# An adaLN block with linear attention and a bilinear GLU on one core: normalised q tiles 5 to 16 turned by VectorE from contiguous runs

## The chip, the cores and the metric

The kernel runs on one core of one Trainium2 chip. The metric is the device time of one execution in microseconds (us); the median of three timed runs of the kernel before is 558.22 us (558.07 to 559.64). Besides, one execution was recorded by the hardware profiler. Engines are named as the profile has them: PE is TensorE (PEld its weight loads), DVE VectorE, ACT ScalarE, POOL GpSimd, SP SyncE, whose queue issues all DMAs of this kernel.

## The reference, cut to what matters

One sequence of S = 2048 tokens with D = 512 columns, 32 heads of 16 columns, F = 1376 hidden columns of the FFN, all in float32:

```python
mod = (silu(c) @ w_mod).reshape(1, 6, 1, -1)          # sa, ca, ga, sb, cb, gb
h = layernorm(x) * (1 + ca) + sa
q, k, v = heads(h @ wqkv)
phi = lambda t: where(t > 0, t + 1, exp(t)) + 1e-6
kv = einsum("bhsd,bhse->bhde", phi(k), v);  z = phi(k).sum(s)
o = (phi(q) @ kv) / (phi(q) . z + 1e-6)
x = x + ga * (o @ wo)
h = layernorm(x) * (1 + cb) + sb
x = x + gb * (((h @ w_gate) * (h @ w_up)) @ w_down)
```

## The kernel before

**Tiling.** The 2048 tokens are 16 tiles of 128 (index i from 0 to 15), four tiles a chunk (`ch`, `NJ` = 4). A tile is 128 tokens on the partitions and 512 columns; the column blocks of 128 are k = 0 to 3 (`KD`). Nearly every buffer is one of 94 of 2 KB a partition (`NB`); of the eight PSUM banks four are of the kind `acc`, four `bank`. Every product is made from a high and a low part of each operand (fp32r), high x high + high x low + low x high, so a product over 512 rows is 12 matmuls of 512 columns.

**Order.** The order of the instructions is written by hand (`manual_schedule`): each engine works its own queue in the order in which the program issues. A helper that is called earlier stands earlier in the queues of all engines that it uses; a `move_in` or `load` stands in SP's queue.

**Stages.** (1) The first layer norm, the modulation and a loop over the 16 tiles that makes k, phi(k) and the sums over the tokens; q products (`proj(i, wq)`) are put between: tiles 0 to 3 in steps 3, 4, 6 and 7, tiles 4 and 5 at the end, tiles 6 to 11 around the matrices that follow. (2) Out of the sums come `wp`, a 512 x 512 matrix that holds k's sums, v and wo and takes phi(q) to the attention's output, and `zb`, the sum of phi(k), broadcast over the partitions. (3) For each tile: `q_a` (ACT) and `q_b` (DVE) make phi(q) (`phq`); `den_p` and `den_r` multiply it by zb and sum each head (`den_a` is both); `den_b` takes a chunk's reciprocals; `den_c` normalises the tile. Then the normalised tile has to be turned, so that its columns lie on the partitions: it is the stationary operand of the product with wp in `y_a`. `turn_h` and `turn_l` make the high and the low part of the turned tile, `y_seed` puts x into a PSUM bank, `y_a` adds 12 matmuls to it, `y_b` takes the sum out, with the statistics of the second norm. `y_step(i)` issues y_a(i), the parts of tile i + 1, the next seed and y_b(i - 1). (4) The FFN: three lone blocks of hidden columns (`gate_up`, `down`), then 18 steps of `block` (seven products `p1`, `p5`, `p6`, `p2`, `p7`, `p3`, `p4`, by sums and differences of token chunks, `Left`, and of weight blocks, `Right`, so that seven products do for eight). `ffn` is a generator; `fill(n)` lets it issue n products. While the first steps run, tiles 14 and 15 are still on their way.

**How a tile is turned.** Tiles 0 to 7: `turn_a`, four TensorE transposes into a PSUM bank (L672). Tiles 8 to 15 (`FLIPPED`): `ready` normalises a tile and stores it to memory (`move_out`), `move_in` loads it again in four pieces so that each partition has what lies in its 32 x 32 blocks, and `turn_v` transposes the 32 x 32 blocks on VectorE (L722). A block takes every fourth word of a row; so the rows of wp for these tiles are those with the same remainder by four (`wp4`), which are made by storing wp to memory (`wp_store`) and loading it in another order (`wp_fetch`). The second norm's chunks 2 and 3 go the same way (`stow`, `unstow`, `flip`, `flipped`), with scales `cb4`, `sb4` and gate and up weights `wg_4`, `wu_4` in that order of rows.

**Names that the change and the prediction touch.** L196 and L197 are the high part (ACT) and the low part (DVE or POOL) of a split; L201 is `split_raw`. L209 to L211 are the matmuls of `product`. L672 is the TensorE transpose, L676 and L680 are turn_h and turn_l, L722 is turn_v, L745 is an extra matmul that opens the bank in y_seed(8, bank), L746 the seed, L755 the matmuls of y_a, L763 and L229 the two halves of y_b for chunk 3. L601 is den_c. L824 is the eviction of `down` on DVE. L896 is flip. L1026 is a matmul of `block`; L1031 is `copy`, by which a block's product starts from another (`copy(b, a)` after p1, without which p6 can't begin). L994 are the sums of Right, L1005, L1008 and L1012 its high and low parts.

Of the kernel before, what the change touches and what calls it, by code (L numbers as in the profile page):

```python
# [11 lines left out]
ALU = mybir.AluOpType  # L12
# [12 lines left out]
def tile_adaln_block(  # L25
# [32 lines left out]
    wu_v = w_up.rearrange("(k p) f -> p k f", p=P)  # L58
    wg_4 = w_gate.rearrange("(p k) f -> p k f", p=P)
    wu_4 = w_up.rearrange("(p k) f -> p k f", p=P)  # L60
    wm_v = w_mod.rearrange("(p k) n -> p k n", k=KD)
# [8 lines left out]
    def f32(ap):  # L70
        return ap.bitcast(F32)
# [141 lines left out]
    def cut(pair, a, b):  # L213
        return pair[0][:, a:b], pair[1][:, a:b]


    class Norm:
# [38 lines left out]
        def xhat(self, *js):  # L256
            for j in js:
                self.n[j] = B("n")
                nc.scalar.activation(self.n[j], self.tiles[j], AF.Identity,  # L259
                                     scale=self.rstd[:, j:j + 1], bias=self.nmr[:, j:j + 1])  # L260

# [239 lines left out]
    for i in range(NT):  # L501
# [13 lines left out]
        if i == 2:  # L515
            turn_x()
            wq.extend(split_raw(r) for r in raw_q)
        if fresh:
# [48 lines left out]
    pzs = {}  # L567
    den0 = consts.tile([P, NH], F32, name="den0")

    def den_z():  # L570

        nc.vector.reduce_sum(den0, zb.rearrange("p (h i) -> p h i", i=DH), axis=AX.X)
        nc.vector.tensor_scalar(den0, den0, EPS_PHI, EPS_DEN, op0=ALU.mult, op1=ALU.add)

    def den_p(ch, *js, on=None):
        for j in js:
            pzs[ch, j] = B("f")
            (on or nc.gpsimd).tensor_tensor(pzs[ch, j], phq[ch * NJ + j], zb, op=ALU.mult)

# [12 lines left out]
    def den_b(ch):  # L592
        nc.vector.tensor_tensor(dens[ch], dens[ch], den0.unsqueeze(1).to_broadcast([P, NJ, NH]), op=ALU.add)
        nc.vector.reciprocal(dens[ch], dens[ch])
# [91 lines left out]

    FLIPPED = range(8, NT)
    SUMS = (0, 1, 2)
    wp4, moved = [], {}

    def wp_store():
        to = [tc.dram_tile([D, D], F32, name=f"wp_{part}") for part in range(2)]
        for g in range(KD):
            for part in range(2):
                nc.sync.dma_start(to[part][g * P:(g + 1) * P], f32(wp[g][part]))
        wp4.append(to)

    def wp_fetch():
        rows = [x.rearrange("(p k) d -> p k d", k=KD) for x in wp4.pop()]
        for k in range(KD):  # L700
            wp4.append((B("w", dt=F32R), B("w", dt=F32R)))
            for part in range(2):
                nc.sync.dma_start(f32(wp4[k][part]), rows[part][:, k])

# [14 lines left out]
    def turn_v(i):  # L719

        tps[i] = B("f")
        nc.vector.transpose(tps[i].rearrange("p (s m i) -> p m s i", m=NQ, i=BL),  # L722
                            moved.pop(i).rearrange("p (m i s) -> p m s i", m=NQ, i=BL))

# [15 lines left out]
    def y_seed(i, of=acc_bank):  # L740

        yps[i] = of()
        if of is bank:

            nc.tensor.matmul(yps[i], wp[0][0][:, :P], wp[0][0], start=True, stop=True)  # L745
        nc.scalar.activation(yps[i], xts[i // NJ][i % NJ], AF.Copy)  # L746

    def y_a(i):
        if i not in yps:
            y_seed(i)  # L750
        pq = pqs.pop(i)
        for k in range(KD):
            (ah, al), (bh, bl) = cut(pq, k * P, (k + 1) * P), (wp4 if i in FLIPPED else wp)[k]
            for x, y in ((ah, bh), (ah, bl), (al, bh)):
                nc.tensor.matmul(yps[i], x, y, start=False, stop=k == KD - 1 and x is al, skip_group_check=True)  # L755
# [10 lines left out]
    def y_step(i, *more, late=(), q=None, turn=True, seed=acc_bank):  # L766
# [6 lines left out]
        if i + 1 in tps:  # L773
            turn_h(i + 1)
            turn_l(i + 1)
        if seed is acc_bank and i + 1 < NT:
            y_seed(i + 1, seed)
# [96 lines left out]

    def by_fours(col, name):

        t, v = consts.tile([P, KD], F32, name=name), tc.dram_tile([D], F32, name=name + "_row")
        nc.sync.dma_start(v.rearrange("(k p) -> p k", p=P), col)
        nc.sync.dma_start(t, v.rearrange("(p k) -> p k", k=KD))
        return t  # L880

    def stow(ch, *js):
# [11 lines left out]
    def flip(ch, *js):  # L894
        for j in js:
            nc.vector.transpose(wide[:, j].rearrange("p (m s i) -> p m s i", m=NQ, i=BL),  # L896
                                blocks.pop((ch, j)).rearrange("p (m i s) -> p m s i", m=NQ, i=BL))

    def flipped(ch, *ks):
        for k in ks:  # L900
            f = B("f")
            nc.scalar.activation(f.rearrange("p (x i) -> p x i", i=BL),
                                 wide.rearrange("p j (m s i) -> p (j m) s i", m=NQ, i=BL)[:, :, k],
                                 AF.Identity, scale=cb4[:, k:k + 1], bias=sb4[:, k:k + 1])
            blocks[ch, "f", k] = f
# [9 lines left out]
    kept = [[tc.dram_tile([P, D], F32, name=f"kept_{ch}_{k}") for k in range(KD)] for ch in PLAIN]  # L915
    cb4, sb4 = by_fours(cb, "cb4"), by_fours(sb, "sb4")
    for ch in range(NCH):
# [62 lines left out]
    class Right:  # L980


        def __init__(self, f, plain):
            f0, self.n = fts[f]
            self.up, self.low = self.tile("raw"), self.tile("raw")
            for t, kh in ((self.up, 0), (self.low, 1)):
                for i, v in enumerate((wg_v, wu_v) if plain else (wg_4, wu_4)):
                    nc.sync.dma_start(t[:, i], v[:, kh * KH:(kh + 1) * KH, f0:f0 + self.n])
# [144 lines left out]
    def right_load(n):  # L1133
        if n < len(steps):
            rights[n] = Right(steps[n][1], steps[n][0][0] in PLAIN)

# [112 lines left out]
    den_a(2, 0, on=nc.vector)  # L1249
    den_c(6)  # L1250
    split_down(f1, nc.gpsimd)
# [34 lines left out]
    ready(12, 13)  # L1286
    g()
    y_step(11, lambda: move_in(12), turn=False, seed=False)
    y_b(11)
# [9 lines left out]
    norm2[2].nmr_of()  # L1299
    norm2[2].xhat(0, 1)  # L1300
    turn_l(12)
    first[0].sum("s1", "s3", on=nc.gpsimd)
    g(lambda: turn_v(13))
    y_seed(13, y_bank)
    norm2[2].xhat(2, 3)
    turn_h(13)
# [44 lines left out]
    fill(1)  # L1351
    norm2[3].xhat(0)
    fill(1)
    norm2[3].xhat(1)
    fill(1)
    norm2[3].xhat(2)
    stow(3, 0, 1)
    fill(1)
    norm2[3].xhat(3)
    stow(3, 2)  # L1360
# [54 lines left out]
```

## Time and profile before

| | before |
|---|---|
| timed runs, median of 3 | 558.22 us (558.07 to 559.64) |
| the profiled execution, whole | 559.39 us |
| its span, first to last instruction | 557.7 us |
| granted TensorE clock, mean | 0.997 |
| instructions | 7356 |

The span is what the profile's views divide; the rest of an execution's time lies around it. A group's row gives how often an instruction ran, its busy time, the mean of one, and the idle time of its engine just before it with what ended it. A window's row gives for each engine its busy time and, in brackets, its number of instructions, then the granted clock, the DMA share and GB/s. A chain's or a timeline's row begins with the start and the duration in us.

### The profile page before, as it was taken

What the parts mean: (1) busy time and instruction counts of PE and PEld (TensorE: products, weight loads), DVE (VectorE), ACT (ScalarE), POOL (GpSimd) and SP (SyncE); (2) the same over time, 40 slices, a digit from 0 to 9 for tenths busy, and PEclk for the clock granted to TensorE, in tenths of its full rate; (3) what the DMA queues carried; (4) which work ended last, traced back from release to release, by engine and by line L of the source; (5) the groups of instructions that cost most, each with busy time, mean ns of one, the idle gap of its engine ahead of it and who ended that gap; (6) DMA issues with size and microseconds to landing.
All of it is one profiled execution on the core that took longest, in us unless ns stands there. A gap on an engine that the chain in (4) does not pass through costs nothing.

```text
span 557.7 us, 7356 instructions
## 1 busy us (share of the span) xinstructions
PE 550.1 (99%) x2505; PEld 451.3 (81%) x2505; DVE 377.8 (68%) x605; ACT 291.4 (52%) x539; POOL 203.0 (36%) x203
## 2 busy tenths in 40 slices
PE   8999999999999999999899999999999999999997
PEld 6888888888888878878688888887888888888886
DVE  7896968977947886877877587886553544434435
ACT  3695856646477567566683545554444444444110
POOL 2000000101012300055698666566667446446200
PEclk9899999999999999999999999999999999999999
DMA  8900203220532605846435162591335222100004
GB/s 279 384 16 2 75 25 103 101 76 1 155 100 92 188 20 169 264 143 162 132 75 148 42 201 65 188 318 29 113 114 150 59 56 58 56 21 0 1 0 150
DMA packets 59141, 60.39 MB, mean 108 GB/s; under 512 B 8608, under 2 KB 37536, under 8 KB 59104
## 3 DMA queue, kind: packets, MB, share of 16 engines
q1 hardware_dynamic: 59104, 59.93, 34.3%
q8 instruction: 19, 0.31, 0.2%
q14 instruction: 18, 0.15, 0.1%
HBM read 43.65 MB, written 16.26 MB: 107 GB/s over the span
## 4 chain that ended last, share of the span: by engine, by line
PE 92%; DVE 3%; ACT 2%; DMA 1%; issue 1%; SPq 0%; DVEq 0%; ACTq 0%
PE bank L1026 32%; PE acc L1106 6%; PE acc L1107 6%; PE acc L1108 6%; PE acc L755 5%; PE bank L209 5%; PE bank L211 5%; PE bank L210 5%; PE acc L351 3%; PE acc L349 3%; PE acc L350 3%; PE bank L839 2%; PE bank L837 2%; PE bank L838 2%; PE bank L272 2%; DMA x<-in_A_x_dram 1%
## 5 line engine op out<-in xcount | busy, mean ns | idle before, releaser
L1026 PE MATMUL bank<-h,w 128*128 128x512 f32 (+1 forms) x798 | 185.4, 390 | 1.5 <-ACT bank L1031 1.5
L1026 PEld LDWEIGHTS bank<-h,w 128*128 128x128 f32 (+1 forms) x798 | 148.1, 186 | 35.8 <-ACT bank L1031 2.6
L1031 ACT ACTIVATE bank<-bank 128x512 f32<-128x512 f32 (+1 forms) x38 | 22.1, 583 | 137.1 <-PE bank L1026 137.0
L824 DVE TENSOR_TENSOR x<-acc,x 128x512 f32<-128x512 f32 (+1 forms) x73 | 48.4, 681 | 47.4 <-PE acc L1108 47.3
L1012 POOL TENSOR_TENSOR w<-raw,w 128x256 fp32r<-128x256 f32 (+3 forms) x38 | 41.3, 1086 | 95.2 <-ACT w L1005 95.2
L1107 PE MATMUL acc<-w,kh 128*128 128x512 f32 (+2 forms) x154 | 59.6, 387 | 0.0
L1106 PE MATMUL acc<-w,kh 128*128 128x512 f32 (+2 forms) x154 | 59.6, 387 | 0.0
L1108 PE MATMUL acc<-w,kl 128*128 128x512 f32 (+2 forms) x154 | 59.5, 386 | 0.0
L197 POOL TENSOR_TENSOR w<-raw,w 128x512 fp32r<-128x512 f32 (+1 forms) x25 | 36.0, 1442 | 55.3 <-ACT w L196 28.5
L250 POOL TENSOR_TENSOR rstd<-ve,half 128x4 f32<-128x4 f32 (+1 forms) x10 | 10.8, 1080 | 120.7 <-DVE ve L249 68.0
L1012 POOL TENSOR_TENSOR w<-t,w 128x512 fp32r<-128x512 f32 (+1 forms) x38 | 49.3, 1320 | 0.0
L197 DVE TENSOR_TENSOR kl<-u,kh 128x512 fp32r<-128x512 f32 (+1 forms) x38 | 26.4, 733 | 30.2 <-ACT kh L196 30.2
L209 PE MATMUL bank<-w,h 128*128 128x512 f32 x104 | 40.8, 392 | 0.0
L211 PE MATMUL bank<-w,h 128*128 128x512 f32 x104 | 40.5, 390 | 0.0
L210 PE MATMUL bank<-w,h 128*128 128x512 f32 x104 | 40.5, 389 | 0.0
L755 PE MATMUL acc<-w,xh 128*128 128x512 f32 x120 | 37.7, 395 | 0.0
L1106 PEld LDWEIGHTS acc<-w,kh 128*128 128x128 f32 (+1 forms) x154 | 28.9, 188 | 6.0
L1108 PEld LDWEIGHTS acc<-w,kl 128*128 128x128 f32 (+1 forms) x154 | 28.9, 188 | 5.9
L1107 PEld LDWEIGHTS acc<-w,kh 128*128 128x128 f32 (+1 forms) x154 | 28.9, 188 | 5.9
L1085 DVE TENSOR_TENSOR u<-bank,u 128x512 f32<-128x512 f32 (+1 forms) x19 | 13.1, 687 | 28.9 <-PE bank L1026 22.9
L259 ACT ACTIVATE n<-x,nmr,rstd 128x512 f32<-128x512 f32 x30 | 22.9, 804 | 12.2 <-DVE nmr L254 12.2
L196 ACT ACTIVATE w<-raw 128x512 fp32r<-128x512 f32 (+2 forms) x44 | 26.3, 619 | 1.9 <-DVE raw L804 1.0
(206 smaller groups left out, 1125.1 us busy)
## 6 DMA issues: line engine op xcount, KB each, us to landing
raw<-in_w_mod_dram SPq DMA_DIRECT2D x24, 256.0 KB, 3.8
raw<-in_B_w_down_dram SPq DMA_DIRECT2D x20, 256.0 KB, 3.2
raw<-in_B_w_gate_dram SPq DMA_DIRECT2D x36, 128.0 KB, 3.7
raw<-in_B_w_up_dram SPq DMA_DIRECT2D x36, 128.0 KB, 3.6
x<-in_A_x_dram SPq DMA_DIRECT2D x16, 256.0 KB, 5.7
out_dram<-x SPq DMA_DIRECT2D x15, 256.0 KB, 2.6
raw<-in_A_wqkv_dram SPq DMA_DIRECT2D x12, 256.0 KB, 5.4
wp<-w SPq DMA_DIRECT2D x8, 256.0 KB, 3.3
```

The lines of the kernel that those rows point to most:

```text
L196: nc.scalar.activation(h, src, AF.Copy)
L197: (low or nc.vector).tensor_tensor(l, src, f32(h), op=ALU.subtract)
L209: nc.tensor.matmul(ps, ah, bh, start=i == 0, stop=False)
L210: nc.tensor.matmul(ps, ah, bl, start=False, stop=False)
L211: nc.tensor.matmul(ps, al, bh, start=False, stop=i == n - 1)
L755: nc.tensor.matmul(yps[i], x, y, start=False, stop=k == KD - 1 and x is al, skip_group_check=True)
L824: nc.vector.tensor_tensor(xt[:, a:b], dn[j][:, a:b], xt[:, a:b], op=ALU.add)
L1012: sub = lambda out, x, y: (on or nc.gpsimd).tensor_tensor(out, x, f32(y), op=ALU.subtract)
L1026: mm = lambda x, y, **kw: nc.tensor.matmul(ps, x[:, k], y, skip_group_check=True, **kw)
L1106: nc.tensor.matmul(ps, hh[:, a:b], dh[:n, c:d], start=i == 0, stop=False)
L1107: nc.tensor.matmul(ps, hh[:, a:b], dl[:n, c:d], start=False, stop=False)
L1108: nc.tensor.matmul(ps, hl[:, a:b], dh[:n, c:d], start=False, stop=i == len(hs) - 1)
```

## The change

It keeps the arithmetic and changes how tiles are turned and in which order work is issued.

- **Block order of the q columns.** The columns of the q weights are put in another order as they are split: `split_blocks` reads the 512 columns as (s, q, i) with i of 32 and writes them as (q, s, i). So phi(q) of a tile comes out with its columns in that order, and the words of a 32 x 32 block are one run of 32 (the transpose in `turn_v` and `flip` reads `(m s i)` where it read `(m i s)`). Tiles 0 to 3, which TensorE still turns, need the plain order: their q products read the weights in runs of 32 (`by_row`), 48 matmuls.
- **Tiles 4 to 7** go the way of tiles 8 to 15: ready, move_in, turn_v (`FLIPPED` now begins at 4). Their 16 TensorE transposes are gone.
- With blocks of whole runs the rows of wp are the plain ones: `wp_store`, `wp_fetch`, `wp4`, `by_fours` with `cb4` and `sb4`, `wg_4` and `wu_4` are gone: 16 + 4 DMA issues. The four tiles bring 4 + 16.
- `zq` and `den0q` are copies of zb and den0 in block order (POOL and DVE, once each), used for tiles from 4 on. The second norm's chunks 2 and 3 are written in block order by `xhat_blocks`.
- The extra matmul in `y_seed(8, bank)` is gone.
- **Order.** Chunk 1's denominators move up into y_steps 1 to 3, its normalisation between the q products of tiles 12 to 15. The parts of tile 6 (counted from 0; the seventh) stand before gate_up's rest. The first Right's sums stand ahead of y_step(11); its parts, and the parts of tiles 14 and 15 and the third sums (s3) of Left, stand ahead of the first block; the eviction of chunk 1's tiles 2 and 3 stands behind the block's fourth product.

```diff
+    def by_block(x):
+        return x.rearrange("p (s q i) -> p q s i", q=NQ, i=BL)
+    def by_row(x):
+        return x.rearrange("p (q s i) -> p s q i", q=NQ, i=BL)
+    def split_blocks(raw):
+        h, l = B("w", dt=F32R), B("w", dt=F32R)
+        view = lambda x: x.rearrange("p (q s i) -> p q s i", q=NQ, i=BL)
+        nc.scalar.activation(view(h), by_block(raw), AF.Copy)
+        nc.vector.tensor_tensor(view(l), by_block(raw), view(f32(h)), op=ALU.subtract)
+        return h, l
...
+        def xhat_blocks(self, *js):
+            for j in js:
+                self.n[j] = B("n")
+                nc.scalar.activation(self.n[j].rearrange("p (q s i) -> p s q i", q=NQ, i=BL),
+                                     self.tiles[j].rearrange("p (s q i) -> p s q i", q=NQ, i=BL), AF.Identity,
                                      scale=self.rstd[:, j:j + 1], bias=self.nmr[:, j:j + 1])
...
-        product(ps, [(cut(norm[ch].t[k], j * P, (j + 1) * P), w[k]) for k in range(KD)])
+        rows = w is wq and i not in FLIPPED
+        product(ps.rearrange("p (s q i) -> p s q i", q=NQ, i=BL) if rows else ps,
+                [(cut(norm[ch].t[k], j * P, (j + 1) * P), tuple(by_row(x) for x in w[k]) if rows else w[k])
+                 for k in range(KD)])
...
+            zq = B("z")
+            nc.gpsimd.tensor_copy(zq.rearrange("p (q s i) -> p q s i", q=NQ, i=BL), by_block(zb))
...
-    FLIPPED = range(8, NT)
+    FLIPPED = range(4, NCH * NJ)
...
         nc.vector.transpose(tps[i].rearrange("p (s m i) -> p m s i", m=NQ, i=BL),
-                            moved.pop(i).rearrange("p (m i s) -> p m s i", m=NQ, i=BL))
+                            moved.pop(i).rearrange("p (m s i) -> p m s i", m=NQ, i=BL))
...
-        if of is bank:
-
-            nc.tensor.matmul(yps[i], wp[0][0][:, :P], wp[0][0], start=True, stop=True)
...
-            (ah, al), (bh, bl) = cut(pq, k * P, (k + 1) * P), (wp4 if i in FLIPPED else wp)[k]
+            (ah, al), (bh, bl) = cut(pq, k * P, (k + 1) * P), wp[k]
...
-    y_step(1)
+    y_step(1, lambda: den_a(1, 0, on=nc.vector))
     y_step(2, lambda: split_gu(f0, nc.gpsimd))
-    y_step(3, lambda: scale_down(f0), wp_store, turn=False, seed=False)
+    den_a(1, 1, on=nc.vector)
+    y_step(3, lambda: scale_down(f0), turn=False, seed=False)
+    den_a(1, 2, 3, on=nc.vector)
+    den_b(1)
     ps12 = proj(12, wq)
     y_b(3)
     norm2[0].rstd_of()
-    den_a(1, 0, on=nc.vector)
+    ready(4)
     q_a(12, ps12)
     ps13 = proj(13, wq)
+    ready(5)
     ln2_nx(0)
     q_b(12)
-    den_a(1, 1, 2, on=nc.vector)
+    ready(6)
+    move_in(4)
     q_a(13, ps13)
     ps14 = proj(14, wq, acc_bank)
     split_down(f0, nc.gpsimd)
-    den_a(1, 3, on=nc.vector)
-    den_b(1)
+    ready(7)
+    move_in(5)
     ln2_turn(0, 0, 1, cast=nc.vector)
     q_b(13)
     ps15 = proj(15, wq, acc_bank)
     ln2_turn(0, 2, 3, cast=nc.vector)
+    move_in(6, 7)
     q_a(14, ps14)
-    den_c(4)
+    split_gu(f1, nc.gpsimd)
+    turn_v(4)
     q_b(14)
     q_a(15, ps15)
-    split_gu(f1, nc.gpsimd)
     g = gate_up(0, f0)
     q_b(15)
-    den_c(5)
+    turn_v(5)
     scale_down(f1)
     g()
-    turn(4)
+    turn_h(4)
+    turn_l(4)
     y_seed(4)
     split_gu(f2)
     g = gate_up(0, f1)
+    turn_v(6)
     den_a(2, 0, on=nc.vector)
-    den_c(6)
     split_down(f1, nc.gpsimd)
     g()
     y_step(4, lambda: scale_down(f2), lambda: den_a(2, 1, on=nc.vector))
     g = gate_up(0, f2)
     split_down(f2)
-    den_c(7)
+    turn_h(6)
+    turn_l(6)
+    y_seed(6)
+    turn_v(7)
+    g()
     den_a(2, 2, on=nc.vector)
-    g()
-    y_step(5, lambda: den_a(2, 3, on=nc.vector), wp_fetch)
+    y_step(5, lambda: den_a(2, 3, on=nc.vector))
...
+    right_sums(0, nc.vector)
     y_step(11, lambda: move_in(12), turn=False, seed=False)
...
     turn_v(14)
-    take = down(1, (2, 3))
+    down_13 = down(1, (2, 3))
     first[1].sum("s1", "s3", "s2", "s4", on=nc.gpsimd)
+    right_split(0)
     y_seed(14, y_bank)
     turn_h(14)
+    turn_v(15)
+    turn_l(14)
+    turn_h(15)
     first[0].split("s1", "s2")
-    turn_l(14)
+    first[1].split("s1", "s2")
     y_b(13)
+    turn_l(15)
+    for x in first:
+        x.split("s3")
+    right_sums(1, nc.vector)
     y_seed(15, y_bank)
-    right_sums(0, nc.vector)
-    take()
-    first[1].split("s1", "s2")
-    turn_v(15)
     for n in range(4):
         banks.append(bank())
-    banks[:] = [banks[n] for n in (2, 0, 1, 3)]
     turn_bank[0] = acc_bank
-    right_split(0)
     draw_load(0)
...
     y_step(14, seed=None)
     fill(1)
     y_b(14)
-    right_sums(1, nc.vector)
-    first[0].split("s3", "s4")
     fill(1)
-    first[1].split("s3", "s4")
+    for x in first:
+        x.split("s4")
     fill(2)
+    down_13()
     y_step(15)
```

More of the change, by code (lines that the diff above doesn't have):

```diff
@@ L259, in xhat @@
                 nc.scalar.activation(self.n[j], self.tiles[j], AF.Identity,
+                                     scale=self.rstd[:, j:j + 1], bias=self.nmr[:, j:j + 1])
+        def xhat_blocks(self, *js):
[3 more added lines that the diff above has]
+                                     self.tiles[j].rearrange("p (s q i) -> p s q i", q=NQ, i=BL), AF.Identity,
                                      scale=self.rstd[:, j:j + 1], bias=self.nmr[:, j:j + 1])
@@ L516, in tile_adaln_block @@
             turn_x()
-            wq.extend(split_raw(r) for r in raw_q)
+            wq.extend(split_blocks(r) for r in raw_q)
         if fresh:
@@ L568, in tile_adaln_block @@
     den0 = consts.tile([P, NH], F32, name="den0")
+    den0q = consts.tile([P, NH], F32, name="den0q")
     def den_z():
@@ L685, in turn @@
         turn_l(i)
-    FLIPPED = range(8, NT)
     SUMS = (0, 1, 2)
[L689 to L703, printed above, removed]
+    moved = {}
     def move_out(*tiles):
@@ L773, in y_step @@
         if i + 1 in tps:
-            turn_h(i + 1)
+            if i + 1 not in pqs:
+                turn_h(i + 1)
             turn_l(i + 1)
-        if seed is acc_bank and i + 1 < NT:
+        if seed is acc_bank and i + 1 < NT and i + 1 not in yps:
             y_seed(i + 1, seed)
@@ L873, in ln2_nx @@
         ln2_xhat(ch)
[L875 to L880, printed above, removed]
     def stow(ch, *js):
@@ L1134, in right_load @@
         if n < len(steps):
-            rights[n] = Right(steps[n][1], steps[n][0][0] in PLAIN)
+            rights[n] = Right(steps[n][1])
     def right_sums(n, on=None):
@@ L1299, in tile_adaln_block @@
     norm2[2].nmr_of()
-    norm2[2].xhat(0, 1)
+    norm2[2].xhat_blocks(0, 1)
     turn_l(12)
@@ L1304, in tile_adaln_block @@
     y_seed(13, y_bank)
-    norm2[2].xhat(2, 3)
+    norm2[2].xhat_blocks(2, 3)
     turn_h(13)
@@ L1351, in tile_adaln_block @@
     fill(1)
-    norm2[3].xhat(0)
+    norm2[3].xhat_blocks(0)
     fill(1)
-    norm2[3].xhat(1)
+    norm2[3].xhat_blocks(1)
     fill(1)
-    norm2[3].xhat(2)
+    norm2[3].xhat_blocks(2)
     stow(3, 0, 1)
     fill(1)
-    norm2[3].xhat(3)
+    norm2[3].xhat_blocks(3)
     stow(3, 2)
```

17 lines of the change are left out of this document (8 added, 9 removed).

## The prediction

> **What bounds the kernel now.** I read the engine shares first, then the share of each engine in the chain of work that ended last.
>
> ```profile
> span 557.7 us, 7356 instructions
> PE 550.1 (99%) x2505; PEld 451.3 (81%) x2505; DVE 377.8 (68%) x605; ACT 291.4 (52%) x539; POOL 203.0 (36%) x203
> PE 92%; DVE 3%; ACT 2%; DMA 1%; issue 1%; SPq 0%; DVEq 0%; ACTq 0%
> ```
>
> TensorE is busy for 550.1 of 557.7 us. A busy bar can hide a bubble, so the pace comes next: 102 matmuls in 23.22 us (chain, below) are 0.2276 us each, while one record lasts 0.39 us, because they overlap. Wherever neighbours start 0.23 us apart TensorE is full, and only two things can move the end: fewer TensorE instructions, or fewer waits in its queue. The waits of TensorE, and the last stretch:
>
> ```profile
> PE acc L148 <- DVE w L143: 2.0, 1, 2.0
> PE bank L1026 <- ACT bank L1031: 1.5, 1, 1.5
> PE bank L279 <- ACT n L259: 0.4, 1, 0.4
> 525.00:558.00 33.00, 29.09 (x135) 24.13 (x133) 15.34 (x24) 4.96 (x9) 1.29 (x1) 1.00 0.18 64
> ```
>
> The first and third waits lie in the first 20 us, and the 3.9 us without TensorE at the end are the last eviction and store; the change touches neither. One wait is left, in the first FFN block at L1026. TensorE's rows there:
>
> ```profile
> 263.59 3.19 PE L1026 MATMUL bank<-h,w 128*128 128x512 f32 x12
> 268.29 3.02 PE L1026 MATMUL bank<-h,w 128*128 128x512 f32 x12 [1.51 <-ACT bank L1031]
> 271.15 0.61 PE L755 MATMUL acc<-w,xh 128*128 128x512 f32 x2
> 274.03 23.22 PE bank L1026 x102
> ```
>
> Twelve matmuls from 263.59 at 0.2276 would let the next start at 266.32; it starts at 268.29. So the hole is 1.97 us by starts, not the 1.51 the wait shows (the last record's overhang hides the rest). The twelve after it take 2.86 us instead of 2.73, another 0.13 for filling the pipe again: **2.10 us** in all.
>
> What ScalarE and VectorE did before it:
>
> ```profile
> 243.35 0.17 DVE L247 TENSOR_SCALAR ve<-sums 128x4 f32<-128x4 f32 x1 [2.11 <-ACT acc L238]
> 256.10 1.10 DVE L722 STREAM_TRANSPOSE f<-u 128x512 f32<-128x512 f32 x1
> 258.42 1.29 DVE L197 TENSOR_TENSOR h<-s,h 128x512 fp32r<-128x512 f32 x2 [1.22 <-ACT h L196]
> 260.24 0.69 DVE L229 BATCH_NORM_STATS2 st<-acc 128x6 f32<-128x512 f32 x1
> 262.50 1.28 DVE L824 TENSOR_TENSOR x<-acc,x 128x512 f32<-128x512 f32 x2
> 263.70 2.38 DVE L197 TENSOR_TENSOR h<-s,h 128x512 fp32r<-128x512 f32 x2
> 266.00 1.08 DVE L722 STREAM_TRANSPOSE f<-u 128x512 f32<-128x512 f32 x1
> 267.12 0.63 ACT L676 ACTIVATE xh<-f 128x512 fp32r<-128x512 f32 x1 [2.61 <-DVE f L722]
> 267.66 0.58 ACT L1031 ACTIVATE bank<-bank 128x512 f32<-128x512 f32 x1
> ```
>
> The copy that TensorE waits for (L1031) had its input at about 265. It stood in ScalarE's queue behind the high part of tile 15 (L676), which waited for tile 15's VectorE transpose (L722 at 266.00), which stood behind four right-hand sums, two evictions (L824) and two low parts (L197) on VectorE.
>
> **The change part by part.**
>
> TensorE transposes of tiles 4 to 7 (L672) and the extra matmul of y_seed(8) go:
>
> ```profile
> 200.51 0.44 PE bank L672 x4
> 200.95 2.76 PE acc L755 x12
> 204.14 5.49 PE acc L755 x24
> 215.64 0.39 PE L745 MATMUL bank<-w 128*128 128x512 f32 x1
> 215.87 0.39 PE L863 MATMUL acc<-w,kh 128*128 128x512 f32 x1
> ```
>
> Four tiles at 0.44 us are 1.76; the lone matmul is the distance 215.64 to 215.87, 0.23. All 17 instructions stand in a stretch where TensorE never waits, so **1.99 us** leave its queue if its inputs keep up.
>
> The hole at 266 to 268: tile 15's transpose now stands right behind tile 14's, before all the low parts; the first right-hand sums move some 20 us ahead to y_step(11), into the 2.11 us that VectorE idles before 243.35; both evictions move behind the block's fourth product. Nothing of tile 15 stands in front of L1031 any more. What is late next is y_seed(15) on ScalarE: it waits for the statistics of tile 13 (L229), behind four low parts. From tile 14's transpose (256.10, with TensorE 1.99 earlier: 254.1) VectorE has two transposes, one low part of a tile, four L197, L229. Bounds: at quick rows (0.69, 0.69, 0.65, 0.69) 5.4 us, ending 259.5; at slow ones (1.10, and 1.19, half of the 2.38, for five low parts, which POOL's work for right_split(0) in its new place may bring) 8.8 us, ending 262.9. Seed and copy at L1031's 0.58 each add 1.2, so the copy is done between 260.7 (then its own input at 263 decides) and 264.1; TensorE needs it at 266.32 - 1.99 = 264.33. The hole closes at both ends, by little at the slow one. I take **2.10 us** gained, and a loss of up to 0.5 for a further slow row as range.
>
> VectorE now turns tiles 4 to 7, and all tiles from contiguous runs instead of every fourth word:
>
> ```profile
> L722 DVE STREAM_TRANSPOSE f<-u 128x512 f32<-128x512 f32 x8 | 8.8, 1097 | 0.0
> L197 DVE TENSOR_TENSOR w<-raw,w 128x512 fp32r<-128x512 f32 x16 | 10.5, 684 | 0.0
> L292 DVE CAST h<-f 128x512 fp32r<-128x512 f32 x19 | 8.0, 419 | 1.6 <-ACT f L284 1.6
> ```
>
> No row shows a contiguous transpose. Bounds: 0.42 us (L292, the quickest pass over 512 columns) and 1.10 (no change). I take 0.69, like every full-rate pass. The Trainium skill, Vector Engine (DVE) Microarchitecture Reference, section Measured stream behaviour on trn2, says that a port keeps full rate only on runs of at least two adjacent words, and gives 1.73 ns a column against 1.054 when one source hops every element; for 512 columns and its 75 ns an estimate from that page is 0.96 against 0.61 us. The 1.10 here fits the hopping kind roughly; the other end no run here shows yet.
>
> Does VectorE keep up with the shorter TensorE stream? The tightest place is tile 7:
>
> ```profile
> 169.07 0.17 DVE L247 TENSOR_SCALAR ve<-sums 128x4 f32<-128x4 f32 x1 [5.02 <-ACT acc L238]
> 180.50:205.70 25.20, 25.20 (x119) 19.83 (x118) 22.45 (x36) 15.20 (x31) 4.81 (x3) 1.00 0.34 104
> 180.50 0.68 DVE L317 SCALAR_TENSOR_TENSOR h<-bank,h 128x512 f32<-128x512 f32 x1
> 183.22 0.68 DVE L601 SCALAR_TENSOR_TENSOR h<-h,den 128x512 f32<-128x512 f32 x1
> 192.65 1.06 DVE L601 SCALAR_TENSOR_TENSOR h<-h,den 128x512 f32<-128x512 f32 x1
> 204.97 0.69 DVE L680 TENSOR_TENSOR xl<-bank,xh 128x512 fp32r<-128x512 f32 x1 [0.32 <-ACT xh L676]
> ```
>
> VectorE is busy 22.45 of 25.2 us here. Tile 7's low part ends at 205.66; its first user is the third matmul of y_a(7), at 204.14 + 14 x 0.229 = 207.35: 1.7 us to spare. TensorE will come 1.76 earlier. VectorE loses four normalisations from this stretch (L601, 0.68 to 1.06, at least 2.7; they move to 169 to 174, where its queue had the denominators, and those move ahead into idle time such as the 5.02 us before 169.07) and q_b(13) (0.68), and gains four transposes, 2.8 (or 4.4). Spare afterwards: 1.7 - 1.76 + 2.7 + 0.68 - 2.8 = 0.5 us, or 1.1 short if the transposes stay at 1.10. I take nothing lost, 1.1 as the other end.
>
> The way through memory: per tile one store and four loads.
>
> ```profile
> moved<-h SPq DMA_DIRECT2D x8, 256.0 KB, 2.1
> u<-moved SPq DMA_DIRECT2D x32, 64.0 KB, 2.0
> 214.82 3.72 SPq L717 DMA_DIRECT2D u<-moved  x8
> 176.95 4.61 SPq L286 DMA_DIRECT2D kept<-f  x4
> ```
>
> Twenty issues come to SyncE's queue; eight stores of wp, its eight loads and four of the column scales go. Tile 4 is normalised right behind L247 at 169.07 and stored near 170; its loads are issued behind tile 6's store, near 173, and at 0.47 us each (3.72 / 8) and 2.0 of landing are in by 177. Its transpose stands where L601 stood at 183.22, behind the modulated blocks: 6 us to spare. Tiles 6 and 7 are issued behind the kept stores, which end at 181.56; eight loads and the landing put them in by 187.3. Tile 6's transpose stands two VectorE passes ahead of its L601 at 192.65, about 191, tile 7's later. They cost nothing; were they late, VectorE's queue would be too, as under the late parts below.
>
> Strided passes elsewhere: split_blocks, xhat_blocks and zq read or write runs of 32 words.
>
> ```profile
> L902 ACT ACTIVATE f<-wide,sb,cb 128x512 f32<-128x512 f32 x8 | 6.4, 806 | 0.7 <-DVE wide L896 0.7
> L259 ACT ACTIVATE n<-x,nmr,rstd 128x512 f32<-128x512 f32 x30 | 22.9, 804 | 12.2 <-DVE nmr L254 12.2
> ```
>
> L902 reads runs of 32 words and costs what the unbroken L259 costs, so these pass at nothing.
>
> Last, TensorE reads the q weights for tiles 0 to 3 in runs of 32 words: 48 matmuls, in no row of before. Bounds: nothing, as on ScalarE (L902), and a factor 1.6, the ratio of hopping to full-rate passes on VectorE (1097 / 684): 48 x 0.2276 x 0.6 = 6.6 us. Runs of 32 are nearer to L902's pattern, the same runs, than to L722's single words: I take 0.
>
> **Sum:** 1.99 + 2.10 = 4.09 us. The profiled span 557.7 becomes 553.6; that execution took 559.39 us, 1.69 around the span, so its like would take 555.3. The three timed runs have the median 558.22, 1.17 below the profiled one; from it: **554.1 us**.
>
> **The rivals.** Changes below 0.3% (1.7 us) can't be told from none.
>
> *Late parts.* VectorE runs behind: tile 7 (up to 1.1) and y_seed(15) (up to 0.5) wait. For it: VectorE at 22.45 of 25.2 us, and transposes of unknown pace. Against it: the lighter queue. 554.1 + 1.6 = 555.7 at worst.
>
> *The hole moves.* Another wait of its size opens between 240 and 275 (tiles 12 and 13 go through memory, VectorE and ScalarE there, and TensorE takes them right after), and only the 1.99 remain: 556.2 us. Against it: that chain starts from TensorE's own products and its transposes are to be quicker.
>
> *Weights in runs slow TensorE* (the other side). Place: proj(0) to proj(3), in steps 3, 4, 6 and 7 of the k loop, where TensorE shows no wait, so each extra is paid whole. At factor 1.6: 554.1 + 6.6 = 560.7 us. It turns the sign from 4.09 / 48 = 0.085 us a matmul on, 0.228 to 0.313. For it: nothing measured. The Trainium skill, Advanced Engine Details and Errata, section Memory Cachelines, warns under PSUM that any non-contiguous pattern slows matmuls significantly; here the output stays contiguous and only the SBUF side hops, where the same section's 16-byte lines would each be read whole. No row here shows such a matmul.
>
> *The transposes gain nothing from contiguous runs*: that part would not do what it says; it is the upper end of the late parts, about 555.5.
>
> **How the numbers follow.** Forecast (553.5 to 555.0) 0.62; late parts, with idle transposes among them, 0.14; the hole moves 0.10; slow weights 0.09; some other loss, such as a buffer released late, 0.05. Faster by over 0.3% is below 556.5: 0.62 + 0.14 + about half of 0.10, 0.81; within, 0.08; slower, 0.11. The range 553.2 to 557.0 takes in late parts and the moved hole; slow weights lie outside it.
>
> **What would show it.** TensorE: 16 transposes fewer at L672, no L745 matmul, no wait at L1026, span near 553.6. VectorE: L722 and L896 near 0.69 us. Starts of the q products of tiles 0 to 3 still 0.23 apart; if they stand at 0.31 or more, the forecast is wrong by sign. A wait of y_a(7) on L680, or of L1026 on L1031, is the late-parts rival. A TensorE busy time that falls by less than 2 us with no wait shown means that I mis-sized the transposes.

## The result and the profile after

| kernel | us, median (range, runs) | ratio to before, 95% interval | profiled span |
|---|---|---|---|
| before, in the same comparison | 558.60 (558.07 to 560.86, 6) | | 557.7 |
| changed | 554.40 (554.28 to 555.40, 6) | 0.9916 [0.9896, 0.9936] | 552.7 |
| changed, second set | 554.37 (554.21 to 554.79, 4) | 0.9922 [0.9907, 0.9937] | 553.1 |
| changed, third set | 554.75 (554.00 to 556.18, 6) | 0.9920 [0.9901, 0.9939] | 554.3 |

Faster, by 4.2 us between the medians; the forecast was 4.09. The page of the changed kernel, its engine shares and the engines' part in the chain that ended last:

```profile
span 552.7 us, 7324 instructions
PE 547.0 (99%) x2488; PEld 449.2 (81%) x2488; DVE 373.6 (68%) x610; ACT 291.7 (53%) x539; POOL 203.4 (37%) x204
PE 99%; DVE 0%; issue 0%
```

17 matmuls fewer (2505 to 2488), and TensorE's share of the chain rises from 92% to 99%. The view of waits has one line left for TensorE (us in total, times, longest), the one in the start-up:

```profile
PE acc L146 <- DVE w L141: 2.0, 1, 2.0
```

The wait of the first block on its copy is gone. Where the time came from is read from starts of the same matmul in both traces. TensorE's timeline in the changed kernel (start, duration):

```profile
27.65 0.39 PE L373 MATMUL acc<-kh,xh 128*128 128x512 f32 x1
...
51.38 0.39 PE L209 MATMUL bank<-w,h 128*128 128x512 f32 x1
51.61 0.40 PE L207 MATMUL bank<-w,h 128*128 128x512 f32 x1
51.84 0.40 PE L208 MATMUL bank<-w,h 128*128 128x512 f32 x1
...
166.86 0.39 PE L207 MATMUL bank<-w,h 128*128 128x512 f32 x1
...
204.64 0.39 PE L766 MATMUL acc<-w,xl 128*128 128x512 f32 x1
...
213.08 0.39 PE L875 MATMUL acc<-w,kh 128*128 128x512 f32 x1
...
260.79 5.60 PE L1030 MATMUL bank<-h,w 128*128 128x512 f32 x24
266.23 0.61 PE L766 MATMUL acc<-w,xh 128*128 128x512 f32 x2
...
548.79 0.28 PE L1112 MATMUL acc<-w,kl 128*128 128x256 f32 x1
```

And those of before that the prediction does not show:

```profile
28.52 0.39 PE L349 MATMUL acc<-kh,xh 128*128 128x512 f32 x1
...
167.34 0.39 PE L209 MATMUL bank<-w,h 128*128 128x512 f32 x1
...
186.86 0.39 PE L838 MATMUL bank<-h,w 128*128 128x512 f32 x1
187.17 0.50 PE L839 MATMUL bank<-h,w 128*128 128x512 f32 x1
187.51 0.39 PE L837 MATMUL bank<-h,w 128*128 128x512 f32 x1
...
553.81 0.28 PE L1108 MATMUL acc<-w,kl 128*128 128x256 f32 x1
```

The differences of these starts make a ledger (the rows at 215.87, 263.59 and 271.15 of before stand in the prediction):

| stretch, named by its ends | before | after | gained |
|---|---|---|---|
| start to the first matmul of step 0 | 28.52 | 27.65 | 0.87 |
| to the q product of tile 12 | 138.82 | 139.21 | -0.39 |
| to the matmul behind y_seed(8) | 48.53 | 46.22 | 2.31 |
| to the first FFN block | 47.72 | 47.71 | 0.01 |
| to the y products behind its second product | 7.56 | 5.44 | 2.12 |
| to the last matmul | 282.66 | 282.56 | 0.10 |

The first line is not taken for the change's. The stretch of 10 to 20 us in three traces (the seventh figure behind the window and its length is TensorE's granted clock): before,

```profile
10.00:20.00 10.00, 9.77 (x51) 8.01 (x52) 8.70 (x18) 8.31 (x14) 0.00 (x0) 0.83 1.05 391
```

the changed kernel,

```profile
10.00:20.00 10.00, 10.00 (x60) 8.28 (x59) 8.68 (x19) 8.30 (x14) 0.00 (x0) 1.00 1.05 392
```

and the changed kernel in its third set:

```profile
10.00:20.00 10.00, 9.14 (x49) 7.45 (x49) 8.14 (x17) 7.59 (x13) 0.00 (x0) 0.83 1.03 374
```

The same kernel was granted 1.00 once and 0.83 another time, and its step 0 then began at 27.65 or at 29.24. So the 5.0 us between the profiled spans hold 0.87 of luck in the start-up, and the ledger without it gives 4.15. From here on kernels are compared by the **stretch** from the first matmul of step 0 to the start of the last matmul, which leaves the start-up out: 525.29 us before, and 521.14, 521.19 and 521.18 in three executions of the changed kernel.

### The profile page after: what moved, and what is told of

The parts are those of the page before. It is cut to its first block, busy times and chain, and to the rows that moved or that the text cites. A ratio compares the mean times of both kernels' runs of the same rounds, so it can differ in the third digit from the quotient of the medians.

```text
span 552.7 us, 7324 instructions
## 1 busy us (share of the span) xinstructions
PE 547.0 (99%) x2488; PEld 449.2 (81%) x2488; DVE 373.6 (68%) x610; ACT 291.7 (53%) x539; POOL 203.4 (37%) x204
## 4 chain that ended last, share of the span: by engine, by line
PE 99%; DVE 0%; issue 0%
PE bank L1030 33%; PE acc L766 7%; PE acc L1110 6%; PE acc L1111 6%; PE acc L1112 6%; PE bank L207 5%; PE bank L209 5%; PE bank L208 5%; PE acc L375 3%; PE acc L374 3%; PE acc L373 3%; PE bank L849 2%; PE bank L851 2%; PE bank L850 2%; PE acc L146 2%; PE bank L293 2%
## 5 line engine op out<-in xcount | busy, mean ns | idle before, releaser
L1035 ACT ACTIVATE bank<-bank 128x512 f32<-128x512 f32 (+1 forms) x38 | 22.2, 583 | 139.6 <-PE bank L1030 139.5
L195 POOL TENSOR_TENSOR w<-raw,w 128x512 fp32r<-128x512 f32 (+1 forms) x25 | 35.1, 1409 | 52.2 <-ACT w L194 47.3
L195 DVE TENSOR_TENSOR kl<-u,kh 128x512 fp32r<-128x512 f32 (+1 forms) x38 | 26.4, 736 | 30.6 <-ACT kh L194 30.6
L998 POOL TENSOR_TENSOR t<-raw,t 128x256 f32<-128x256 f32 (+1 forms) x34 | 25.9, 761 | 1.4
L766 PEld LDWEIGHTS acc<-w,xh 128*128 128x128 f32 x120 | 22.2, 188 | 4.6
```

The lines of the kernel that those rows point to most:

```text
L195: (low or nc.vector).tensor_tensor(l, src, f32(h), op=ALU.subtract)
L998: sub = lambda out, x, y: (on or nc.gpsimd).tensor_tensor(out, x, y, op=ALU.subtract)
```

## The experiments

**The old late order in the changed kernel.** Everything between y_step(11) and the first block as before:

```diff
-    right_sums(0, nc.vector)
     y_step(11, lambda: move_in(12), turn=False, seed=False)
...
-    down_13 = down(1, (2, 3))
+    take = down(1, (2, 3))
...
     y_seed(15, y_bank)
+    right_sums(0, nc.vector)
+    take()
+    first[1].split("s1", "s2")
+    turn_v(15)
```

> The changed kernel, with the work from y_step(11) to the first FFN block in the order of before (first right-hand sums, low parts, evictions, tile 15's transpose and right_split(0) at their old places). Theory (the order of that work closes the hole before p6): the wait of L1026's line on the copy comes back. Two of the transposes in the chain to it are 0.4 us quicker each than before, so the hole should be about 1.97 - 0.8 = 1.2 us, and with the refill of the pipe the time about 1.3 us above the changed kernel's 554.4: 555.7. Rival (the quicker transposes close it, the order does nothing): no wait, 554.4.

Measured: 556.49 us (555.79 to 557.59, 6 runs), ratio 0.9950 [0.9931, 0.9968]; the stretch is 522.61, 1.47 longer. TensorE's timeline in it (in brackets the idle time before and what ended it):

```profile
261.82 2.43 PE L1030 MATMUL bank<-h,w 128*128 128x512 f32 x10
264.90 3.06 PE L1030 MATMUL bank<-h,w 128*128 128x512 f32 x12 [0.65 <-ACT bank L1035]
267.80 0.62 PE L766 MATMUL acc<-w,xh 128*128 128x512 f32 x2
...
270.52 2.88 PE L1030 MATMUL bank<-h,w 128*128 128x512 f32 x12
273.58 2.81 PE L1030 MATMUL bank<-h,w 128*128 128x512 f32 x11 [0.18 <-DVE u L1089]
```

From 261.82 to 267.80, 22 matmuls take 5.98 us where 22 x 0.2276 is 5.01: 0.97 lost at the old place. From 270.52, twelve take 3.06 instead of 2.73, and filling the pipe again brings that to about 0.45. So with quick transposes alone the old order still loses what it lost, less a third, and part of it one wait further on: the order is needed. The chain is the one that the prediction read from the kernel before: ScalarE's high part of tile 15 waits 2.23 us for VectorE's transpose and starts at 263.74, and the copy stands right behind it at 264.27.

**The new late order alone, in the kernel before.** The same edit the other way round:

```diff
+    right_sums(0, nc.vector)
     y_step(11, lambda: move_in(12), turn=False, seed=False)
...
+    turn_v(15)
+    turn_l(14)
+    turn_h(15)
...
-    right_sums(0, nc.vector)
-    take()
...
     fill(2)
+    down_13()
     y_step(15)
```

> The kernel before, with only the work from y_step(11) to the first FFN block in the new order; tiles 4 to 7 are still turned by TensorE and VectorE's transposes still read every fourth word. Theory: the hole of 1.97 us and its refill close but for a few tenths, since tile 14's and 15's transposes are 0.4 us longer each and y_seed(15) stands right before the copy: 1.6 to 2.1 us below before, 556.5 to 557.0 where before has 558.6. Rival (the quicker transposes close it): the hole stays, 558.6 or little less.

Measured: 556.88 us (556.25 to 557.81, 7 runs), ratio 0.9960 [0.9945, 0.9976]; stretch 523.06, 2.23 below before. TensorE's timeline:

```profile
263.76 5.60 PE L1026 MATMUL bank<-h,w 128*128 128x512 f32 x24
269.20 0.62 PE L755 MATMUL acc<-w,xh 128*128 128x512 f32 x2
```

24 matmuls without a break, 5.44 us to the next product where before took 7.56: the whole 2.12 with the slow transposes still in place. Order alone closes the hole, and it needs nothing of the other edits. Its moves went in together, so what each is worth alone isn't shown.

**All VectorE transposes strided again.** Their input is read at every fourth word:

```diff
-                            moved.pop(i).rearrange("p (m s i) -> p m s i", m=NQ, i=BL))
+                            moved.pop(i).rearrange("p (m i s) -> p m s i", m=NQ, i=BL))
```

> The changed kernel, with every transpose on VectorE reading every fourth word again (20 instructions, 1.10 us in place of 0.70); the words come out in another order, so the tiles from 4 on and chunks 2 and 3 of the second norm are scrambled. Theory: TensorE waits in two places only, for tile 7's low part (0.32 us to spare now, four transposes of 0.4 us more in front of it: up to 1.3 us) and before p6 (0.58 us to spare, two transposes and the low parts: up to 0.3 us): 555.4 to 556.0. Rival (VectorE's pace is off TensorE's path): 554.4.

Measured: 554.99 us (554.76 to 555.70, 6 runs), ratio 0.9925 [0.9909, 0.9940]; stretch 521.59, only 0.45 longer: a miss, I had expected 555.4 to 556.0. The transposes were slow as meant; VectorE's groups by form (busy us, mean ns), first of this kernel, then of the changed one:

```profile
L736 DVE STREAM_TRANSPOSE f<-u 128x512 f32<-128x512 f32 x12 | 13.0, 1091 | 0.8 <-DMA u<-moved 0.8
L901 DVE STREAM_TRANSPOSE wide<-u 128x512 f32<-128x512 f32 x8 | 8.6, 1086 | 0.0
```

```profile
L736 DVE STREAM_TRANSPOSE f<-u 128x512 f32<-128x512 f32 x12 | 8.4, 702 | 0.9 <-DMA u<-moved 0.9
L901 DVE STREAM_TRANSPOSE wide<-u 128x512 f32<-128x512 f32 x8 | 5.5, 699 | 0.0
```

But 7.7 us more of VectorE (13.0 + 8.6 - 8.4 - 5.5) reached TensorE in one place, at tile 7's low part. VectorE's row there, then TensorE's:

```profile
205.05 0.68 DVE L709 TENSOR_TENSOR xl<-f,xh 128x512 fp32r<-128x512 f32 x1
```

```profile
205.07 0.61 PE L766 MATMUL acc<-w,xh 128*128 128x512 f32 x2
205.79 0.50 PE L766 MATMUL acc<-w,xl 128*128 128x512 f32 x1
206.13 0.62 PE L766 MATMUL acc<-w,xh 128*128 128x512 f32 x2
```

The low part ends at 205.73, the matmul was due at 205.07 + 2 x 0.2276 = 205.53 and starts at 205.79; with the late one behind it, 0.26 + 0.11 = 0.37. The view of waits has no line for it. In the changed kernel VectorE idles for 0.37 us just before 199.0 (waiting for TensorE's phi product); in this run there is no idle time at that place (the row starts at 200.46 right behind the transpose), so the gap took up part of the extra work.

**Tiles 4 to 7 by TensorE again** (counted from 0; the title counts from one). This kernel has no extra matmul in y_seed(8), and its output is off by a relative error of 0.021, which the run after this one takes up:

```diff
-    FLIPPED = range(4, NCH * NJ)
+    FLIPPED = range(8, NCH * NJ)
...
-    turn_h(6)
-    turn_l(6)
+    turn(6)
     y_seed(6)
-    turn_v(7)
```

> The changed kernel, with tiles 4 to 7 turned by TensorE again; their q products then read the weights in runs of 32 words too, 48 more matmuls. Theory (TensorE's own instructions are the time): 4 x 0.44 = 1.76 us for the transposes and 48 x 6.7 ns = 0.32 for the runs, 2.1 us above the changed kernel: 556.5. Rival (the transposes were hidden behind other work, and the gain came from the hole and elsewhere): under 0.8 us above, 555.2 or less.

Measured: 557.89 us (557.36 to 559.40, 12 runs), ratio 0.9978 [0.9967, 0.9989]; stretch 524.32, 3.17 longer, 1.1 more than the 2.1 expected. TensorE's timeline has the surplus:

```profile
207.89 0.61 PE L766 MATMUL acc<-w,xh 128*128 128x512 f32 x2
209.12 0.50 PE L766 MATMUL acc<-w,xl 128*128 128x512 f32 x1 [0.61 <-DVE xl L709]
209.46 0.63 PE L766 MATMUL acc<-w,xh 128*128 128x512 f32 x2
```

Due at 207.89 + 0.455 = 208.35, it starts at 209.12: 0.77, and 0.11 to refill. In the new order tile 7's parts stand behind chunk 2's denominators on VectorE, and a transpose by TensorE only comes just before its parts. With 1.76 for the 16 transposes and 0.32 for 48 more q matmuls in runs (below) that makes 2.96; where the last 0.2 goes was not followed up.

**The same, with the extra matmul of y_seed(8) back:**

```diff
         yps[i] = of()
+        if of is bank:
+            nc.tensor.matmul(yps[i], wp[0][0][:, :P], wp[0][0], start=True, stop=True)
```

> e4_tensor_turns with the extra matmul of y_seed(8) put back. Theory (the transposes of 128 columns leave the bank's other columns set to be overwritten, so the matmul was there to make y_a add to the seed of x): the output is the reference's again, and the time is 0.23 us above e4_tensor_turns. Rival (the deviation of e4 has another cause): it stays.

Measured in a single execution: 557.72 us, stretch 524.50, 0.18 above the last. The matmul costs about what a matmul costs (0.23 by starts), and with it the output is the reference's again. So with tiles 4 to 7 turned by TensorE the seed of tile 8 needs the extra matmul, and with these tiles turned by VectorE the changed kernel can leave it out. That the state which the transposes leave in the bank is the reason is the theory above; no run looks at the bank itself.

**How short may a run of the q weights be?** Tiles 0, 1, 2 and 3 read them in runs of 32, 8, 2 and 1 words, and their products are written to PSUM in the same runs:

```diff
-        product(ps.rearrange("p (s q i) -> p s q i", q=NQ, i=BL) if rows else ps,
...
+        if w is wq and i not in FLIPPED:
+            n = {0: 32, 1: 8, 2: 2, 3: 1}[i]
+            runs = lambda x: x.rearrange("p (q s i) -> p s q i", s=4, i=n)
+            product(ps.rearrange("p (q s i) -> p s q i", s=4, i=n),
```

In the changed kernel the output `ps` is written unbroken (the view of `(s q i)` as s, q, i keeps the order in memory). Here its view is that of the weights. So the edit changes two things at once, the reading of the weights and the writing of the output, and tile 0's columns come out in another order too; the expectation below speaks of the weights alone.

> The changed kernel, in which the q products of tiles 0 to 3 read the weights as the moving operand in runs of 32, 8, 2 and 1 words (tile by tile; a jump after each run); the columns of tiles 1 to 3 come out in another order, so their attention is scrambled. The changed kernel's trace has 233.3 ns a matmul with runs of 32 against 226.7 unbroken, 6.7 ns for 16 runs. Theory A (one cycle for each run): 0.42 ns a run, so 253 ns at runs of 8 (64 runs), 333 at 2 (256 runs), 440 at 1 (512 runs). Theory B (a line of 16 bytes is read whole, a jump costs nothing by itself): 233 at runs of 32 and 8, and a rise only at runs of 2 and 1. Time: under A some 5 us more than the changed kernel (12 matmuls each by 20, 100 and 207 ns make 4 us), less under B.

Measured in a single execution: 560.88 us, stretch 526.62, 5.47 longer. TensorE's timeline where the product of tile 2 begins:

```profile
68.13 0.62 PE L207 MATMUL bank<-w,h 128*128 128x512 f32 x1
68.57 0.64 PE L208 MATMUL bank<-w,h 128*128 128x512 f32 x1
69.03 0.64 PE L209 MATMUL bank<-w,h 128*128 128x512 f32 x1
```

From the second on, starts are 0.46 us apart, a factor 2.03. Tile 3, at single words, has 0.46 too; tile 1, at runs of 8, 2.54 us for eleven steps, 0.231; tile 0, at runs of 32, 0.233, as in the changed kernel, where only the weights are read in runs. Theory A, a price per jump (253, 333 and 440 ns for 8, 2 and 1 words), falls. Theory B has the pattern right, no price at 8 and a rise at 2 and 1, but not the size: the time rose by more than under A. Somewhere between 8 words and 2 there is a step, and on either side of it the length hardly counts. Whether the weights or the output cost the factor of 2 no run here separates.

**Tile 3 by VectorE too,** its normalisation with tile 0's:

```diff
-    FLIPPED = range(4, NCH * NJ)
+    FLIPPED = range(3, NCH * NJ)
...
-    den_c(0)
+    den_c(0, 3)
     w_out(2, 3)
...
+    move_out(3)
+    move_in(3)
     turn_a(0)
```

> The changed kernel with tile 3 too turned by VectorE (normalised together with tile 0, through memory, its q weights read unbroken). Theory (TensorE's own stream is the time): 0.44 us for its four transposes and 12 x 6.7 ns = 0.08 for the reading, 0.52 us below the changed kernel in the same call. Rival (its way through memory is late for y_a(3), or the earlier normalisation delays wp): a wait at y_a(0) or y_a(3), same time as the changed kernel or above.

Measured: 554.73 us (553.67 to 555.46, 4 runs), ratio 0.9926 [0.9911, 0.9941], like the changed kernel run beside it (554.37). The stretch is 520.87, 0.28 shorter where 0.52 was expected: from the matmul ahead of tile 0's transposes to the second one behind them TensorE takes 1.22 us instead of 0.91, as w_out's work now stands behind one normalisation more in VectorE's queue. The run behind the next one tests that.

**Tiles 2 and 3.** The edit is the last one with `range(2, ...)` and `den_c(0, 2, 3)`; besides, `q_b(9)` moves behind `turn_l(0)`.

> The changed kernel with tiles 2 and 3 turned by VectorE. Theory: twice the gain of tile 3 alone, 1.04 us below the changed kernel, if VectorE finishes tile 0's low part in time: its queue has 1.2 us more in front of it at 150 to 156. Rival: TensorE waits at y_a(0) for tile 0's low part or at y_a(2) for tile 2's way through memory (stored near 152, in by 158, wanted at 160), and the gain is eaten: 554 or above.

Measured: 554.55 us (554.48 to 555.28, 4 runs), ratio 0.9928 [0.9911, 0.9944]; stretch 521.09, 0.05 shorter instead of 1.04. Here the profile has a wait of TensorE, and VectorE's timeline shows what stood in front:

```profile
PE bank L701 <- DVE n L645: 0.5, 1, 0.5
```

```profile
149.30 1.89 DVE L631 SCALAR_TENSOR_TENSOR h<-h,den 128x512 f32<-128x512 f32 x3
151.11 1.28 DVE L645 TENSOR_TENSOR n<-bank,row 128x512 f32<-128x512 f32 x2
```

Three normalisations (L631) ahead of w_out's L645 instead of one hold up the transposes of tile 0. By starts these come 0.67 us late (150.95 to 151.85, where 0.23 is the step) and tile 1's 0.23 late (155.07 to 155.53): 0.9 of the 1.04 expected. Work taken from TensorE is given back as a wait, because its preparation came too early in another queue.

**Tile 3, normalised behind w_out:**

```diff
     w_out(2, 3)
+    den_c(3)
     q_b(9)
```

> As e6_tile3, with tile 3 normalised behind w_out(2, 3) instead of in front of it. In e6's trace TensorE lost 0.2 us at tile 0's transposes, since tile 3's normalisation stood in front of w_out's products in VectorE's queue. Theory: that loss goes and tile 3 still comes back in time (in by about 160, wanted at 163): 0.52 us below the changed kernel of this call by the starts of TensorE's instructions, 553.9 by the clock. Rival: tile 3 is late at y_a(3), TensorE waits there, no gain.

> The changed kernel again, beside e9_tile3_later on the same chip: 554.4 us.

Measured: 554.14 us (553.77 to 555.43, 6 runs), ratio 0.9911 [0.9892, 0.9930], against 554.75 and 0.9920 [0.9901, 0.9939] for the changed kernel beside it. The medians are 0.6 apart and the intervals overlap, so the times do not tell them apart; the stretch, 520.80 against 521.18, is 0.38 shorter of the 0.52 expected. At tile 0's transposes TensorE takes 0.90 us again, so the loss there did come from the normalisation; tile 1's now start 0.12 late (154.07 to 154.43). It is the shortest stretch of all kernels here. The changed kernel's run in an earlier set is this one:

> The changed kernel itself, to stand beside the other runs of this call on the same chip: 554.4 us as before, within the half microsecond by which the clock in the first 20 us shifts single executions.

It gave the second set of the first table.

## Why the prediction was right

**Transposes and the extra matmul: 1.99 forecast, 2.31 in the ledger.** Before also had two small hitches at gate_up(0, f1): its rows at 186.86, 187.17 and 187.51 start 0.31 and 0.34 apart instead of 0.23; 0.2 lost in all. The view of waits has no line for them, but GpSimd's row in before, which makes low parts of f1's weights, shows what came late:

```profile
184.12 3.00 POOL L197 TENSOR_TENSOR w<-raw,w 128x512 fp32r<-128x512 f32 x2 [6.74 <-ACT w L196]
```

It ends at 187.12, and the late matmul starts 0.05 behind it. With the new late order alone, which leaves this place as it was, the row ends at 187.29 and the late matmul starts at 187.35. In the changed kernel `split_gu(f1, nc.gpsimd)` is called earlier, the row ends at 185.26, and the same matmul starts at 186.16 without a hitch. So this 0.2 comes from an order that the prediction gave no price, which leaves about 2.1 for the transposes and the matmul. The two kernels with TensorE's transposes back agree: by starts each tile's four transposes cost 0.44 to 0.46 there, 1.8 for four tiles within a loss of 3.17, and the matmul cost 0.18.

**The hole: 2.10 forecast, 2.12 measured,** and by its order, as the new order alone shows. One reading of it was wrong: the prediction puts all that the shown 1.51 lacks of 1.97 on the last record's overhang. That is 0.16 (0.39 less 0.23). About 0.29 lies earlier, inside the first twelve matmuls. GpSimd and TensorE in before:

```profile
263.73 1.81 POOL L1012 TENSOR_TENSOR w<-t,w 128x512 fp32r<-128x512 f32 x1
265.59 0.96 PE L1026 MATMUL bank<-h,w 128*128 128x512 f32 x3
```

The ninth matmul was due at 263.59 + 8 x 0.2276 = 265.41, starts at 265.59, 0.05 behind the end of GpSimd's row, and the next start is 0.11 late. It is the third of p5, the first to use that low part of Right. So the hole was two waits, and the new order also moves up `right_split(0)`, which makes this low part.

The chain that I priced ran otherwise, too. VectorE and ScalarE in the changed kernel:

```profile
252.92 1.30 DVE L736 STREAM_TRANSPOSE f<-u 128x512 f32<-128x512 f32 x2
254.40 0.83 DVE L709 TENSOR_TENSOR xl<-f,xh 128x512 fp32r<-128x512 f32 x1 [0.17 <-ACT xh L705]
255.44 5.49 DVE L195 TENSOR_TENSOR h<-s,h 128x512 fp32r<-128x512 f32 x4 [0.21 <-ACT h L194]
260.86 0.69 DVE L242 BATCH_NORM_STATS2 st<-acc 128x6 f32<-128x512 f32 x1
```

```profile
261.58 0.60 ACT L757 ACTIVATE acc<-x 128x512 f32<-128x512 f32 x1 [3.08 <-DVE st L242]
262.35 0.58 ACT L1035 ACTIVATE bank<-bank 128x512 f32<-128x512 f32 x1 [0.17 <-PE bank L1030]
```

The four low parts (L195) took 5.49 / 4 = 1.37 us each, over my slow bound of 1.19, with POOL's right parts beside them. Quick transposes and an earlier start paid for it: the copy (L1035) is done at 262.93, between the forecast's 260.7 and 264.1, and the matmul that needs it starts 12 x 0.2276 behind 260.79, at 263.52. The copy even waited 0.17 for its own input. So my estimate of the chain was short in one row, and 0.6 us were left to spare where its slow end left 0.2.

**Contiguous transposes: 0.69 forecast, 0.70 measured,** at 1.09 strided. The Trainium skill, Vector Engine (DVE) Microarchitecture Reference, section Measured stream behaviour on trn2, led to estimates of 0.61 and 0.96: both some 0.1 low, with the ratio of 1.57 against 1.55 measured.

**Tile 7: 0.5 us to spare forecast, 0.32 found.** VectorE's row in the changed kernel:

```profile
203.64 0.68 DVE L709 TENSOR_TENSOR xl<-f,xh 128x512 fp32r<-128x512 f32 x1
```

It ends at 204.32, and TensorE's row at 204.64 is its first user. The place was right, and it was the one that gave when the transposes were slowed. The price was not: for strided transposes I had 1.1 us there and 1.6 with y_seed(15), and 0.37 and nothing were measured. I had added four times 0.4 us to a queue as if it had no gaps.

**The way through memory and ScalarE's passes over runs of 32 at nothing:** right. The loads of the tiles (count, size, median us to landing) and the passes of ScalarE that write runs of 32 in the changed kernel:

```profile
u<-moved SPq DMA_DIRECT2D x48, 64.0 KB, 2.0
```

```profile
L279 ACT ACTIVATE n<-x,nmr,rstd 128x512 f32<-128x512 f32 x8 | 6.2, 804 | 0.0
```

The landing time is that of before with half as many transfers again, and the pass costs the 804 ns of the unbroken one.

**Weights in runs: 0 forecast, 0.32 measured.** In TensorE's timeline above, the unbroken product ends at 51.61, and from there starts are 0.233 apart instead of 0.227. 48 x 6.7 ns is 0.32 of the 0.39 that the second line of the ledger loses. The sign of the rival was right, its size not: its condition (0.085 us a matmul) is missed by a factor of 13 at runs of 32, and is met at runs of 2 with the output in the same runs, where 48 such matmuls would lose 48 x 0.234 = 11.2 us. The Trainium skill, Advanced Engine Details and Errata, section Memory Cachelines, warns under PSUM of slow matmuls for any non-contiguous pattern. The run lengths above do not bear that out for an output in runs of 32 or 8 words (0.233 and 0.231 us), and at runs of 2 and 1 they can't tell the output from the weights.

So the sum, 1.99 + 2.10 = 4.09, stands against 4.15 in the ledger, but not by each term: 0.39 lost that I had at nothing, 0.42 gained that I hadn't seen (0.2 of hitches, 0.1 more in the same stretch and 0.10 of another hitch at 296). That the two nearly cancel is luck; the two terms themselves were met by their mechanisms.

## What to carry to other kernels

Where TensorE is full, count its instructions and its holes by starts, since only these move the end: a quarter of the tiles' transposes, and the place of a few instructions on other engines, were worth 2 us each, while 7.7 us of VectorE were worth 0.45. A layout change that gives one engine contiguous runs gives another broken ones: ask how long a run is, not only whether it is broken. And work moved off the bounding engine pays only if its preparation isn't put in front of that engine's next input: with tiles 2 and 3 moved as well, nearly all of the 1.04 us taken from TensorE came back as waits.

## What the runs showed of the hardware

- A matmul of 512 fp32r columns starts every 227 ns with an unbroken moving operand, and every 233 with it in runs of 32 words. With the moving operand and the output both in runs it was 233 at runs of 32, 231 at 8, and 460 at 2 and at single words 16 bytes apart; which of the two costs the 460 isn't shown.
- The granted clock between 10 and 20 us was 1.00 or 0.83 in executions of one kernel, and its step 0 began at 27.65, 28.03 or 29.24 us: a difference of 1.6 us that a comparison of single profiles would give to the change. Over all thirteen profiles here step 0 began at 27.32 to 28.26 us in the seven with 1.00, and at 28.52 to 29.24 in the six with 0.83.
- A subtraction of 128x512 on VectorE with both sources in SBUF took 0.69 us, and 1.37 with POOL at work beside it (four in a row at 255.44 in the changed kernel; 1.08 for the same four with the new late order alone). That POOL is the cause was not tried.
- A matmul's record lasts 0.39 us where starts are 0.23 apart, so the view of waits shows less than TensorE loses, and some waits not at all: 0.37 us at tile 7 in the strided kernel, and 0.2 and 0.29 at the hitches of before, can be seen from starts alone.
